# Delta-rule attention and two MLPs on one core: K and q of the first chunks loaded in natural layout and transposed by quadrants, norms in fewer instructions, a new order

## The chip, the cores and the metric

The kernel runs on one core of a Trainium2 chip. The time is that of one execution in device microseconds, from launch to end; the median of several runs is given. Lower is better.

## The reference

Three parts follow each other. The first is an attention with a state that a delta rule updates, for 4 batches of 8 heads, 768 tokens, head dimension 48:

```python
k_n = k / (np.linalg.norm(k, axis=-1, keepdims=True) + 1e-06)
for t in range(S):
    kt, vt, bt = (k_n[:, :, t], v[:, :, t], beta[:, :, t, None])
    y[:, :, t] = np.einsum('bhd,bhde->bhe', q[:, :, t], state)
    v_old = np.einsum('bhde,bhd->bhe', state, kt)
    state = state + bt[:, :, :, None] * np.einsum('bhd,bhe->bhde', kt, vt - v_old)
```

Its output, 3072 tokens of 384 values, goes through two MLPs (384 to 2048 to 384): the first with a quadratic bend between -1 and 1 in place of a ReLU, the second with h * clip(h + 3, 0, 6) / 6. All is float32.

## The kernel before

The 768 tokens are cut into 12 chunks of 64. For a chunk, all 32 (batch, head) pairs are worked on at once; they lie on two halves of the partitions, 16 units u in each half. `front(c)` (L1465) does what does not need the state: it loads K in natural layout into KN[c % 2] (`load_kv`, L847), computes the norms (`norms`, L872), brings K and q into the transposed layout (KTT, QQ), multiplies K by K and by q (`products`, L942), inverts the triangular matrix of the chunk (`inverse`, L1003) and scales V. `chain(c)` (L1133) then takes the state: it subtracts what the state holds already (K times state), applies the inverse (E, G), adds to the state (E, KN: the last reader of KN[c % 2]) and makes y, whose two halves, high and low part, go to XB for the MLP. A float32 product on TensorE is done as two matrix instructions; the MLPs split each operand into a high and a low part and do three products.

For chunks 0 to 3 (c < ct = 4) the transposed layout of K and q is made by TensorE. `load_tok` (L800) loads K a second time and q into padded buffers ST (for chunks 0 and 1 also into four buffers that lie in G, cleared by `zero`), two transfers of 96 KB for each half hb. `transposes` (L914) then turns 128 tokens and pairs at once: four instructions of `nc.tensor.transpose` against the identity IDN, for each of K and q and of two hb; ScalarE or VectorE copies the bank to KTT or QQ. From chunk 4 on, `block_transposes` (L827) does it on VectorE from STB, which lies in the same memory as ST.

The inverse ends in a forward substitution: `steps` (L1018) issues two small instructions for each of 15 rows (31 from chunk 4 on), `TMP = TL * DL` (L1029) and `TL = TL - TMP` (L1034), one after another. Whether VectorE or GpSimd takes them is set by `tpool`, which lists chunks 2 to 11.

`wload` (L1276) converts the weights of an MLP block f from HBM words into a high and a low part (L1313 to L1325), some on ScalarE, some on VectorE, a few on GpSimd. MLP block 0 works on chunk 0 alone, block 1 on chunk 1, each later block on two chunks. `mg` says how many weight blocks block 0 is ahead before block 1 is interleaved.

Nothing runs in the order of the text. `Plan.op` records every operation with an assumed duration and a priority, `Plan.emit` (L341) simulates the engines and picks an order from the priorities, and `rearrange` (L590) then moves single operations to other places (`MOVES`) and other engines (`TAKEN`). The priority of a stage of a chunk is

```python
def pri(c, name):
    return c + PR[name] - (PR["first"] if c == 0 else 0) + (PR["off"][c] if c < len(PR["off"]) else 0) + PR["pg"].get((c, name), 0)
```

and the lower one goes first. `hyst` is the time in nanoseconds for which the simulation holds quadrant work (products of 64 x 64 or 32 x 32 tiles) back so that two such groups can stand together; groups named in `urg` (inverse, state update, u, y) are not held. Where TensorE waits in the opening, the plan fills it with products that nobody reads (`fill`, on GH).

Of the kernel before, what the change touches and what calls it, by code (L numbers as in the profile page):

```python
# [19 lines left out]
RATIO = 0.0672  # L20
# [3 lines left out]
PR = dict(tl=53.380307, tp=0.183739, pk=1,  # L24
          pg={(0, 'chain'): 15.406015, (0, 'inv'): -0.97796, (0, 'kv'): -3.174274, (0, 'lv'): 1.308145, (0, 'norm'): 1.19811, (0, 'pm'): -0.151105,
              (0, 'prod'): 0.777632, (0, 'tok'): -0.552347, (0, 'tr'): 1.012284, (0, 'y'): -0.443861, (1, 'chain'): 0.042635, (1, 'inv'): -1.23228,
# [17 lines left out]
          dx=0.998118, sx=65.747392, dl=753.315017, ms=('act', 'dve'), wd=4, fm=-64.663392, aw=('act', 'dve', 'pool'), mg=10, fl=4553.24511,  # L44
          off=(-9.521246, 4.24236, 3.60679, -11.476239), mb=(29.802453, -3.591307), slots=2, fast=(0,), slate=0, mk=0, hm=303.25043, kv=-20.5097,
          tok=-4.956834, norm=-3.403349, tr=-1.523895, prod=7.676092, pm=9.657382, inv=-7.144682, sv=17.887724, w=-1.449, chain=2.315386, y=0.495043,
          wl=6.676133, wls=0.156421, mp=-1.413011, lv=-24.378343, first=-2.104309, bias=-134.594302, fill=3000,
# [4 lines left out]
MOVES = ((19, 0), (18, 19), (11, 18), (78, 11), (20, 78), (12, 20), (21, 12), (58, 82), (38, 5), (83, 38), (39, 83), (6, 17), (56, 6), (22, 56),
# [1662 lines left out]
```

## Time and profile before

| | us |
|---|---|
| median of 3 runs | 1007.03 |
| lowest and highest run | 1006.11, 1007.99 |
| profiled execution | 1007.33 |
| its span, first to last instruction | 1005.50 |
| TensorE busy in the span | 968.4 |
| VectorE, ScalarE, GpSimd busy | 613.6, 483.5, 299.8 |

The profiled execution is the one that the rows below come from; 1.83 us of its time lie outside the span. The busy time of TensorE covers its matrix instructions with modelled ends, and an engine's share over the whole span mixes an opening, in which weights are converted and the first chunks prepared, with a long stretch of MLP work. [...]

### The profile page before, as it was taken

How to read it: one execution, taken by the hardware profiler on the slowest of the kernel's cores; microseconds unless marked ns; L12 is line 12 of the kernel's file. 1: busy time of each engine (PE TensorE's matmuls, PEld its weight loads, DVE VectorE, ACT ScalarE, POOL GpSimd, SP SyncE). 2: the span in 40 equal slices, each digit the busy share in tenths (PEclk: the TensorE clock that was granted, in tenths of full speed). 3: DMA queues.
4: the chain of work that ended last, by engine and by line, in shares of the span. 5: the costliest groups of instructions: out<-in, count | busy, mean ns of one | idle time of the engine just before them, and what ended most of it. 6: DMA issues, size and time to landing. Idle time of an engine off the chain costs nothing.

```text
span 1005.5 us, 27383 instructions
## 1 busy us (share of the span) xinstructions
PE 968.4 (96%) x11540; PEld 834.8 (83%) x11540; DVE 613.6 (61%) x1161; ACT 483.5 (48%) x934; POOL 299.8 (30%) x663
## 2 busy tenths in 40 slices
PE   5788899999999999999999999999999999999998
PEld 4667889978777887887887888998989898989998
DVE  4999788887778687778555886434242324242422
ACT  5769666556455465544436774323232323232422
POOL 2112443758557685685811110210000000000000
PEclk9768999999999999999999999999999999999999
DMA  7774433433333233222023665003200200200000
GB/s 152 190 189 115 105 80 64 79 54 57 52 86 58 43 51 93 39 45 70 20 97 102 214 194 157 1 1 95 63 32 1 63 32 14 66 16 1 33 1 32
DMA packets 208460, 71.78 MB, mean 71 GB/s; under 512 B 154960, under 2 KB 204240, under 8 KB 208336
## 3 DMA queue, kind: packets, MB, share of 16 engines
q1 hardware_dynamic: 205376, 69.44, 28.8%
q8 instruction: 90, 1.47, 0.6%
q10 hardware_dynamic: 2960, 0.59, 0.3%
q14 instruction: 34, 0.28, 0.1%
HBM read 53.68 MB, written 14.16 MB: 67 GB/s over the span
## 4 chain that ended last, share of the span: by engine, by line
PE 84%; DVE 7%; ACT 4%; DMA 2%; issue 1%; SPq 1%; POOL 0%; ACTq 0%; DVEq 0%; POOLq 0%
PE bank L759 84%; DVE TBS L1313 1%; DMA RAWL<-in_moe_w_out_dram 1%; DVE WLA L717 1%; ACT TBS L1316 1%; ACT GF L1377 0%; DVE GF L1379 0%; ACT GF L1378 0%; DVE RAWL L1319 0%; DMA KN<-in_k_dram 0%; DVE KQ L1319 0%; ACT WLA L728 0%; DVE TL L1034 0%; DVE SM L884 0%; DMA RAWR<-in_moe_w_out_dram 0%
## 5 line engine op out<-in xcount | busy, mean ns | idle before, releaser
L759 PE MATMUL bank<-XB,WLA 128*128 128x512 f32 (+1 forms) x1404 | 327.7, 380 | 4.8 <-ACT GF L1377 2.7
L759 PEld LDWEIGHTS bank<-XB,WLA 128*128 128x128 f32 x1404 | 250.1, 190 | 55.0 <-DVE GF L1379 6.1
L1383 DVE SCALAR_TENSOR_TENSOR GF<-GF,bank 128x512 f32<-128x512 f32 x96 | 66.0, 688 | 159.6 <-ACT GF L1382 159.6
L1382 ACT ACTIVATE GF<-bank 128x512 f32<-128x512 f32 x96 | 57.4, 599 | 171.2 <-PE bank L759 161.7
L1029 POOL TENSOR_TENSOR TMP<-TL,DL 128x126 f32<-128x126 f32 (+25 forms) x278 | 111.4, 401 | 60.6 <-DVE DL L1087 34.1
L1034 POOL TENSOR_TENSOR TL<-TL,TMP 128x126 f32<-128x126 f32 (+25 forms) x278 | 118.0, 425 | 21.7
L759 PE MATMUL bank<-GH,WLA 128*128 128x512 f32 (+1 forms) x504 | 120.0, 366 | 1.4 <-ACT RAWR L728 1.4
L759 PE MATMUL bank<-XB,WLB 128*128 128x512 f32 (+1 forms) x468 | 109.3, 377 | 0.5 <-DVE GF L1379 0.3
L728 ACT ACTIVATE GH<-GF 128x512 fp32r<-128x512 f32 (+1 forms) x120 | 69.0, 578 | 74.5 <-DVE GF L1379 38.2
L759 PEld LDWEIGHTS bank<-GH,WLA 128*128 128x128 f32 x504 | 87.0, 191 | 16.3 <-ACT RAWR L728 1.6
L759 PEld LDWEIGHTS bank<-XB,WLB 128*128 128x128 f32 x468 | 83.2, 188 | 16.3 <-DVE GF L1379 0.7
L1377 ACT ACTIVATE GF<-bank 128x512 f32<-128x512 f32 (+1 forms) x112 | 59.5, 532 | 74.8 <-PE bank L759 61.6
L717 DVE TENSOR_TENSOR GL<-GF,GH 128x512 fp32r<-128x512 f32 (+1 forms) x109 | 72.3, 664 | 34.5 <-ACT GH L728 26.9
L1379 DVE SCALAR_TENSOR_TENSOR GF<-bank,GF 128x512 f32<-128x512 f32 (+1 forms) x112 | 67.8, 609 | 38.3 <-ACT GF L1378 34.5
L1378 ACT ACTIVATE GF<-GF 128x512 f32<-128x512 f32 (+1 forms) x112 | 63.4, 568 | 2.6
L759 PE MATMUL bank<-GL,WLA 128*128 128x512 f32 (+1 forms) x252 | 64.6, 366 | 0.0
L717 POOL TENSOR_TENSOR GL<-GF,GH 128x512 fp32r<-128x512 f32 (+1 forms) x27 | 30.6, 1132 | 103.5 <-ACT GH L728 83.5
L759 PEld LDWEIGHTS bank<-GL,WLA 128*128 128x128 f32 x252 | 43.8, 190 | 7.2
L759 PE MATMUL bank<-WLA,GH 128*128 128x384 f32 x220 | 46.6, 349 | 3.1 <-ACT WLA L728 3.1
L759 PEld LDWEIGHTS bank<-WLA,GH 128*128 128x128 f32 x220 | 39.9, 193 | 5.3 <-ACT WLA L728 3.9
L759 PE MATMUL bank<-GH,WLB 128*128 128x512 f32 (+1 forms) x168 | 39.0, 363 | 0.0
L759 PEld LDWEIGHTS bank<-KQ 48*64 48x64 f32 x1152 | 28.5, 152 | 9.5 <-ACT KQ L728 3.9
(196 smaller groups left out, 1431.0 us busy)
## 6 DMA issues: line engine op xcount, KB each, us to landing
XB<-X SPq DMA_DIRECT2D x36, 256.0 KB, 4.4
X<-XB SPq DMA_DIRECT2D x30, 256.0 KB, 2.5
KQ<-in_moe_w_out_dram SPq DMA_DIRECT2D x16, 384.0 KB, 4.1
KQ<-in_moe_w_in_dram SPq DMA_DIRECT2D x16, 384.0 KB, 4.7
KN<-in_k_dram SPq DMA_DIRECT2D x24, 192.0 KB, 3.6
RAWL<-in_moe_w_out_dram SPq DMA_DIRECT2D x12, 384.0 KB, 5.4
out_dram<-E SPq DMA_DIRECT2D x24, 192.0 KB, 1.9
RAWL<-in_moe_w_in_dram SPq DMA_DIRECT2D x24, 144.0 KB, 3.9
```

The costliest lines, as they stand in the source:

```text
L717: alts[e] = (d, lambda e=e: ENG[e].tensor_tensor(out=val(out), in0=val(in0), in1=val(in1), op=op))
L728: lambda: nc.scalar.activation(out=val(out), in_=val(in_), func=AF.Copy, scale=scale))
L759: nc.tensor.matmul(o, l, r, start=start, stop=stop, skip_group_check=skip)
L1029: P.op(te, d, lambda t=t, s=s, r0=r0, a0=a0, a1=a1, m=m: ve.tensor_tensor(out=t[:, a0:a1], in0=TL[:, r0 + a0:r0 + a1, s:s + 1].to_broadcas ...
L1034: P.op(te, d, lambda t=t, s=s, r0=r0, a0=a0, a1=a1: ve.tensor_tensor(out=TL[:, r0 + a0:r0 + a1, 0:s], in0=TL[:, r0 + a0:r0 + a1, 0:s], in1 ...
L1313: P.op("dve", 67 + 0.53 * n, lambda s_=s_, hw=hw: W.tensor_scalar(out=s_, in0=hw, scalar1=-2147483648, scalar2=None, op0=ALU.bitwise_and), ...
L1316: P.op("act", 166 + n, lambda s_=s_, lw=lw: nc.scalar.activation(out=s_.bitcast(I16).rearrange("p (n t) -> p t n", t=2)[:, 0], in_=lw.bitc ...
L1377: P.op("act", da, lambda: nc.scalar.activation(out=gf, in_=ps, func=AF.Relu, scale=0.5, bias=0.5), r=hkeys(hb, hv), w=gk, prio=mp)
L1378: P.op("act", da + 48, lambda: nc.scalar.activation(out=gf, in_=gf, func=AF.Square), w=gk, r=gk, prio=mp)
L1379: P.op("dve", 1.06 * n + 60, lambda: nc.vector.scalar_tensor_tensor(out=gf, in0=ps, scalar=1.0, in1=gf, op0=ALU.max, op1=ALU.min), r=hkeys ...
L1382: P.op("act", da, lambda: nc.scalar.activation(out=gf, in_=ps, func=AF.Relu, scale=1.0 / 6.0, bias=0.5), r=hkeys(hb, hv), w=gk, prio=mp)
L1383: P.op("dve", 1.06 * n + 60, lambda: nc.vector.scalar_tensor_tensor(out=gf, in0=gf, scalar=1.0, in1=ps, op0=ALU.min, op1=ALU.mult), r=hkey ...
```

## The change

The second load of K is gone. K is read out of KN, which the norms and the state update use too, and q is loaded in the same natural layout into QN: for chunks 0 and 1 into the memory of G, for chunks 2 and 3 into that of ST. `transposes` multiplies quadrants of 64 x 64 by a quadrant of the identity, 16 products for a call and two more where the last unit has no 64 columns. The condition `c < PR["ct"]` is as before, so this holds for chunks 0 to 3. The norms take the root with a bias in place of a maximum, and a Relu on ScalarE stands for two steps on VectorE. The clearing of the four buffers is gone. All settings, MOVES and TAKEN are from a new search; among them tpool now lists chunks 0 and 1 too, and hyst, mg and the priorities differ.

```diff
-RATIO = 0.0672
+RATIO = 0.08603
...
-          tok=-4.956834, norm=-3.403349, tr=-1.523895, prod=7.676092, pm=9.657382, inv=-7.144682, sv=17.887724, w=-1.449, chain=2.315386, y=0.495043,
-          wl=6.676133, wls=0.156421, mp=-1.413011, lv=-24.378343, first=-2.104309, bias=-134.594302, fill=3000,
-          tpool=(2, 3, 4, 5, 6, 7, 8, 9, 10, 11), hc=1, halves=1, biasa=873.603855, b16=(0, 1, 2, 3), hyst=1599.18963, fgap=589.297285, me=300,
...
+          aw=('act', 'dve', 'pool'), mg=12, fl=5004.56908, off=(0.407006, 1.099343, -4.45226, -17.582803), mb=(30.430605, -8.43156), slots=2,
+          fast=(0,), slate=0, mk=0, hm=3.441689, kv=-22.656238, tok=-1.658581, norm=-5.921339, tr=-7.667599, prod=-5.210624, pm=1.784778,
+          inv=-4.833225, sv=23.14785, w=-1.449, chain=14.336995, y=7.703994, wl=4.177815, wls=0.059205, mp=-7.898513, lv=-19.500437, first=14.033467,
+          bias=-130.893752, fill=3000, tpool=(0, 1, 2, 3, 4, 5, 6, 7, 8, 9, 10, 11), hc=1, halves=1, biasa=873.608597, b16=(0, 1, 2, 3),
+          hyst=9693.5056, fgap=513.276091, me=10, c3=('act', 'pool'), back=19928.2499, dh=100, margin=0.001, umargin=244.041264,
...
-    extra = [gw[:, 512 * i:512 * i + 512] for i in range(4)]
-    ST += [x.rearrange("p (a x) -> p a x", a=NP) for x in extra]
+    QN = [x.rearrange("p (u d) -> p u d", d=D) for x in (gw[:, 0:U * D], gw[:, 1024:1024 + U * D], ST2.rearrange("p n a x -> p (n a x)")[:, 0:U * D])]
...
-    def load_tok(c, hb, src):
...
+    def load_q(c):
+        P.tag = f"tok c{c} q"
+        for dl in range(2):
+            act = c == 0
+            P.dma(lambda dl=dl, act=act: (nc.scalar if act else nc.sync).dma_start(out=QN[min(c, 2)][SH[dl]], in_=nat(q, c, dl)), CH * U, CH * U * D * 4, eng="act" if act else "sp",
...
-        P.op("dve", 82, lambda: W.tensor_scalar_max(s(1), s(0), 1e-30), r=["sm0"], w=["sm1"], prio=pr, port=("dve",))
-        P.op("act", 200, lambda: nc.scalar.activation(out=s(2), in_=s(1), func=AF.Sqrt), r=["sm1"], w=["sm2"], prio=pr)
+        P.op("act", 200, lambda: nc.scalar.activation(out=s(2), in_=s(0), func=AF.Sqrt, scale=1.0, bias=1e-30), r=["sm0"], w=["sm2"], prio=pr)
         P.op("dve", 170, lambda: W.reciprocal(out=s(3), in_=s(2)), r=["sm2"], w=["sm3"], prio=pr)
-        P.op("dve", 82, lambda: W.tensor_tensor(out=s(4), in0=s(1), in1=s(3), op=ALU.mult), r=["sm1", "sm3"], w=["sm4"], prio=pr, port=("dve",))
-        P.op("dve", 82, lambda: W.tensor_tensor(out=s(5), in0=s(2), in1=s(4), op=ALU.add), r=["sm2", "sm4"], w=["sm5"], prio=pr, port=("dve",))
-        P.op("dve", 82, lambda: W.tensor_scalar(out=NRM[st], in0=s(5), scalar1=0.5, scalar2=1e-6, op0=ALU.mult, op1=ALU.add),
-             r=["sm5"], w=[("nrm", st)], prio=pr, port=("dve",))
+        P.op("act", 130, lambda: nc.scalar.activation(out=s(5), in_=s(2), func=AF.Relu, scale=0.5, bias=1e-6), r=["sm2"], w=["sm5"], prio=pr)
+        P.op("dve", 82, lambda: W.scalar_tensor_tensor(out=s(4), in0=s(0), scalar=0.5, in1=s(3), op0=ALU.mult, op1=ALU.mult), r=["sm0", "sm3"], w=["sm4"], prio=pr, port=("dve",))
+        P.op("dve", 82, lambda: W.tensor_tensor(out=NRM[st], in0=s(5), in1=s(4), op=ALU.add), r=["sm5", "sm4"], w=[("nrm", st)], prio=pr, port=("dve",))
...
-    def transposes(c, hb, i, is_k):
+    def transposes(c, hb, is_k):
...
+        src, nm, x = (KN[st], "kn", st) if is_k else (QN[min(c, 2)], "qn", min(c, 2))
+        flat = src.rearrange("p u d -> p (u d)")
         def pe():
-            for p in range(NP):
-                nc.tensor.transpose(bk.tile[0:112, p * 128:(p + 1) * 128], ST[i][:, p, 0:112], IDN)
+            for a in range(NP):
+                for g in range(2):
+                    for dl in range(2):
+                        o = a * 128 + g * CH
+                        x0 = D * (g * NK + hb * NP + a)
+                        x1 = min(x0, U * D - 64)
+                        mm(bk.tile[SH[dl], o:o + CH], flat[SH[dl], x1:x1 + 64], IDN[SH[dl], SH[dl]])
+                        if x1 < x0:
+                            mm(bk.tile[HD[dl], o:o + CH], flat[SH[dl], x0:x0 + D], IDN[SH[dl], SH[dl]])
...
+        if c < PR["ct"]:
+            load_q(c)
         for hb in range(2):
             if c < PR["ct"]:
-                ik = load_tok(c, hb, k)
-                iq = load_tok(c, hb, q)
-                transposes(c, hb, ik, True)
-                transposes(c, hb, iq, False)
+                transposes(c, hb, True)
+                transposes(c, hb, False)
             products(c, hb)
...
-    for i in range(4):
-        zero(ST[2 + i], [("st", 2 + i)], 470)
```

## Rows read from the trace of the kernel before

**Rows 1.** Windows of the whole core; after the stretch, its length, each engine busy (instructions)

```profile
0.00:67.05 67.05, 45.87 (x969) 36.93 (x969) 52.19 (x155) 41.45 (x84) 10.82 (x30) 0.78 0.74 170
67.05:128.00 60.95, 51.29 (x1291) 47.28 (x1290) 53.69 (x116) 47.04 (x99) 21.10 (x44) 0.88 0.54 124
128.00:600.00 472.00, 469.20 (x7248) 384.77 (x7248) 360.62 (x670) 265.43 (x539) 258.08 (x582) 1.00 0.35 80
600.00:1005.50 405.50, 402.01 (x2034) 365.87 (x2034) 147.09 (x222) 129.56 (x215) 9.78 (x7) 1.00 0.12 38
```

**Rows 2.** The chain of waits, first 30 us: start, length, what

```profile
4.46 4.41 DMA KN<-in_k_dram
```

**Rows 3.** Timeline of all engines, first 20 us: start, length, engine, line, operation, count

```profile
11.18 0.83 ACT L878 ACTIVATE X<-KN 128x768 f32<-128x768 f32 x1
...
14.24 0.17 DVE L889 TENSOR_TENSOR SM<-SM 128x16 f32<-128x16 f32 x1
...
14.45 0.18 DVE L890 TENSOR_TENSOR SM<-SM 128x16 f32<-128x16 f32 x1
...
14.46 3.72 PE L759 MATMUL bank<-KQ 48*64 48x128 f32 x96 [2.52 <-DVE SM L889]
...
16.90 0.42 DVE L966 TENSOR_TENSOR X<-bank,ND 128x256 f32<-128x256 f32 x1 [0.29 <-ACT KQ L974]
```

**Rows 4.** Timeline of TensorE, first 200 us

```profile
8.90 2.19 PE L921 MATMUL bank<-IDN,G 128*112 128x128 f32 x8 [0.92 <-DMA G<-in_k_dram]
...
20.74 0.62 PE L921 MATMUL bank<-IDN,G 128*112 128x128 f32 x4
...
40.62 1.10 PE L921 MATMUL bank<-IDN,ST 128*112 128x128 f32 x4
...
54.67 2.03 PE L759 MATMUL bank<-E,KN 64*48 64x48 f32 x64
...
67.05 4.48 PE L759 MATMUL bank<-XB,WLA 128*128 128x256 f32 x18
...
100.19 2.90 PE L759 MATMUL bank<-KQ,E 48*48 48x64 f32 x128
...
106.18 0.94 PE L759 MATMUL bank<-E,KN 64*48 64x48 f32 x64 [1.08 <-DVE YS L1248]
...
147.97 2.03 PE L759 MATMUL bank<-KQ,E 48*48 48x64 f32 x128
```

**Rows 5.** Timeline of TensorE, 300 to 390 us

```profile
303.24 0.97 PE L759 MATMUL bank<-GL,WLA 128*128 128x512 f32 x3
...
329.70 0.84 PE L759 MATMUL bank<-GL,WLA 128*128 128x512 f32 x3
```

**Rows 6.** Windows of VectorE, instructions on TMP alone

```profile
0.00:67.05 67.05, 11.67 (x53) 0.78 0.74 170
...
sum 1005.50, DVE 12.98; mean DVE 3.25
```

**Rows 7.** Timelines of VectorE and GpSimd, first and last substitution steps

```profile
23.23 0.17 DVE L1029 TENSOR_TENSOR TMP<-TL,DL 128x15 f32<-128x15 f32 x1
...
34.61 1.03 DVE L1034 TENSOR_TENSOR TL<-TL,TMP 128x15 f32<-128x15 f32 x1
...
53.49 0.18 DVE L1029 TENSOR_TENSOR TMP<-TL,DL 128x15 f32<-128x15 f32 x1
...
71.24 0.18 DVE L1034 TENSOR_TENSOR TL<-TL,TMP 128x15 f32<-128x15 f32 x1
...
34.52 1.07 POOL L717 TENSOR_TENSOR WLA<-RAWL,WLA 128x384 fp32r<-128x384 f32 x1 [5.12 <-ACT WLA L728]
...
103.48 0.33 POOL L1029 TENSOR_TENSOR TMP<-TL,DL 128x15 f32<-128x15 f32 x1 [4.27 <-DVE DL L1058]
...
115.55 0.23 POOL L1034 TENSOR_TENSOR TL<-TL,TMP 128x15 f32<-128x15 f32 x1
```

More of the change, by code (lines that the diff above doesn't have):

```diff
@@ L52 @@
[L52 removed]
[226 rows of a table removed]
[L279 to L283 removed]
+PR = dict(tl=293.787129, tp=4.414826, pk=1,
+          pg={(0, 'inv'): 1.288053, (0, 'kv'): 0.012598, (0, 'lv'): 0.099566, (0, 'norm'): 0.108177, (0, 'pm'): 0.514614, (0, 'prod'): -0.32987,
+              (0, 'sv'): 1.411888, (0, 'tok'): -0.072668, (0, 'tr'): -1.082274, (0, 'y'): -0.781211, (1, 'kv'): 1.47192, (1, 'lv'): -0.339201,
+              (1, 'norm'): -0.136947, (1, 'prod'): 0.637285, (1, 'tok'): 0.268505, (1, 'tr'): 0.19817, (10, 'chain'): -0.961739,
[5 rows of a table added]
+              (2, 'prod'): -0.173157, (2, 'tok'): 0.350917, (2, 'tr'): -0.823694, (2, 'y'): -1.283838, (3, 'chain'): 0.413498, (3, 'inv'): -2.52562,
+              (3, 'norm'): 0.386412, (3, 'pm'): -1.27796, (3, 'prod'): 1.357839, (3, 'sv'): 1.063503, (3, 'tok'): 0.428693, (4, 'chain'): -1.120612,
[9 rows of a table added]
+              (9, 'tr'): 2.980542, (9, 'y'): 0.26363}, dx=1.022497, sx=41.802129, dl=318.887832, ms=('act', 'dve'), wd=4, fm=9941.86254,
+          aw=('act', 'dve', 'pool'), mg=12, fl=5004.56908, off=(0.407006, 1.099343, -4.45226, -17.582803), mb=(30.430605, -8.43156), slots=2,
[3 more added lines that the diff above has]
+          hyst=9693.5056, fgap=513.276091, me=10, c3=('act', 'pool'), back=19928.2499, dh=100, margin=0.001, umargin=244.041264,
+          urg=('inv', 's', 'u', 'y'), sw=(217, 95), ad=('act', 'dve'), dp=('dve',), ct=4, dg=('dve', 'pool'), dw=('dve', 'pool'), pq=190)
@@ new lines @@
+MOVES = ((4, 0), (6, 4), (12, 6), (5, 12), (18, 5), (7, 18), (66, 3), (14, 66), (131, 14), (34, 131), (187, 11), (13, 187), (525, 13), (383, 33),
[227 rows of a table added]
+TAKEN = dict(dve=(36, 49, 52, 157, 176, 352, 359, 492, 500, 605, 611, 616, 757, 779, 979, 1131, 1156, 1158, 1302, 1305, 1307, 1437, 1501, 1649, 1650,
+             1679, 1822, 1958, 2184, 2207, 2377, 2490, 2643, 2711, 2815, 2885, 2886, 2888, 3022, 3033, 3055, 3066, 3093, 3097, 3101, 3246, 3248,
+             3263, 3269, 3286, 3295, 3320, 3331, 3342, 3353, 3386, 3397, 3452, 3497, 3542, 3554, 3560, 3578, 3616, 3723,), pool=(32, 37, 50, 181,
+             194, 379, 747, 780, 902, 1041, 1043, 1048, 1185, 1339, 1700, 1713, 2232, 2234, 2480, 2593, 2765, 2924, 3012, 3034, 3056, 3287, 3310,
+             3398, 3420, 3453, 3510, 3564, 3600, 3608, 3609, 3639, 3674, 3684, 3694, 3724, 3754, 3764,))
@@ L795, in zero @@
         P.op("pool", dur, lambda: nc.gpsimd.memset(ap, 0.0), w=keys)
-    stage = [0]
-    def load_tok(c, hb, src):
-        P.tag = f"tok c{c} h{hb}"
-        if c < 2:
-            i = (0 if hb == 0 else 2 + 2 * c) + stage[0] % 2
-        else:
-            i = stage[0] % NST
-        stage[0] += 1
-        for b in range(2):
-            ap = src[2 * b + hb, :, c * CH:(c + 1) * CH, :].rearrange("h s d -> s h d")
-            dst = ST[i][64 * b:64 * b + 64].rearrange("p a (e x) -> p (a e) x", e=2)[:, :, 0:D]
-            act = c == 0 and hb == 1
-            P.dma(lambda ap=ap, dst=dst, act=act: (nc.scalar if act else nc.sync).dma_start(out=dst, in_=ap), CH * H, CH * DM * 4, eng="act" if act else "sp",
-                  w=[("st", i, b)], r=[("st", i)], prio=pri(c, "tok") - (0.01 if c == 0 and hb == 0 else 0.0), bulk=c > 0)
-        return i
+    def load_q(c):
[3 more added lines that the diff above has]
+            P.dma(lambda dl=dl, act=act: (nc.scalar if act else nc.sync).dma_start(out=QN[min(c, 2)][SH[dl]], in_=nat(q, c, dl)), CH * U, CH * U * D * 4, eng="act" if act else "sp",
+                  w=[("qn", min(c, 2), dl)], pre=[("st", 0), ("st", 1)] + [("stb", d, f, t) for d in range(2) for f in range(2) for t in range(2)] if c >= 2 else [], prio=pri(c, "tok"), bulk=c > 0)
     def load_blocks(c, src, nm):
@@ L824, in load_blocks @@
                     P.dma(lambda ap=ap, dst=dst: nc.sync.dma_start(out=dst, in_=ap), 32 * U, 32 * U * 4 * n,
-                          si=490, w=[("stb", dl, f, th)], pre=[("st", i, b) for i in range(2) for b in range(2)], prio=pri(c, "tok"), bulk=True)
+                          si=490, w=[("stb", dl, f, th)], pre=[("qn", 2, dl) for dl in range(2)] + [("st", 0), ("st", 1)], prio=pri(c, "tok"), bulk=True)
     def block_transposes(c):
@@ L918, in transposes @@
         pr = pri(c, "tr")
+        src, nm, x = (KN[st], "kn", st) if is_k else (QN[min(c, 2)], "qn", min(c, 2))
+        flat = src.rearrange("p u d -> p (u d)")
         def pe():
-            for p in range(NP):
-                nc.tensor.transpose(bk.tile[0:112, p * 128:(p + 1) * 128], ST[i][:, p, 0:112], IDN)
+            for a in range(NP):
[7 more added lines that the diff above has]
+                            mm(bk.tile[HD[dl], o:o + CH], flat[SH[dl], x0:x0 + D], IDN[SH[dl], SH[dl]])
         if is_k:
-            P.op("pe", 400, pe, load=0.85, ni=8, r=[("st", i, 0), ("st", i, 1), "idn"], w=[bk], pre=[("kt", st, hb)], alloc=bk, prio=pr)
+            P.op("pe", 880, pe, load=0.6, ni=64, tiled=True, r=[(nm, x, 0), (nm, x, 1), "idn"], w=[bk], pre=[("kt", st, hb)], alloc=bk, prio=pr)
             ks = slice(hb * NP, (hb + 1) * NP)
@@ L929, in transposes @@
         else:
-            P.op("pe", 400, pe, load=0.85, ni=8, r=[("st", i, 0), ("st", i, 1), "idn"], w=[bk], pre=[("qt", st, hb)], alloc=bk, prio=pr)
+            P.op("pe", 880, pe, load=0.6, ni=64, tiled=True, r=[(nm, x, 0), (nm, x, 1), "idn"], w=[bk], pre=[("qt", st, hb)], alloc=bk, prio=pr)
             o = QQ[st][0:112].rearrange("p (b h a) s -> p h a b s", b=2, h=2)[:, hb]
@@ L1096, in inverse @@
         P.op("dve", 620, lambda: nc.vector.transpose(out=NH, in_=TT), r=["dl"], w=["nh"], prio=pr)
-        early_st = [("st", 2 + 2 * st + i, b) for i in range(2) for b in range(2)] if c < 2 else []
+        early_st = [("qn", c, dl) for dl in range(2)] if c < 2 else []
         for g in range(2):
```

13 lines of the change are left out of this document (removed), and 483 rows, old and new, of tables (MOVES, pg).

## The prediction

> **What bounds it now.** I read the windows first, cut at the first MLP product and at the point from which TensorE stays full [rows 1]. From 128 us to the end TensorE is busy 871.21 of 877.5 us at full granted clock, so there the time is its work and nothing else: only fewer or shorter TensorE instructions help. Ahead of 128 us it sits idle 21.18 + 9.66 = 30.8 us, and the mean clock is 0.78 and 0.88 of full. In that opening VectorE is the fullest engine, 105.88 of 128 us, with ScalarE at 88.49. The reader is to see two regimes. In the opening, the chain of chunk 0 and the conversion of the weights share VectorE and ScalarE, and what comes sooner there shifts the full stretch forward. Behind it, every TensorE instruction added costs its length.
>
> The chain of waits and the timeline then show the first microseconds. The second half of K for the norms is on that chain until 8.87 us [rows 2]. The square starts at 11.18, the products at 14.46 and the scaling of X at 16.90 [rows 3]. On TensorE the first MLP product is at 67.05 us, so chunk 0 needs 50 us from X to there [rows 4].
>
> **What the change does to this, step by step.** The sum is made against the profiled execution: span 1005.50 us, 1007.33 with what lies around it, 0.30 over the median of 1007.03.
>
> *Loads.* The second reading of K goes, 16 transfers of 96 KB (64 x 8 rows of 192 B, four a chunk); q comes in half as many, twice as large. For chunk 0, that leaves four transfers in place of ten ahead of the products. K could land some 2 to 2.4 us sooner if its second half is issued at about 2 us and takes the 4.41 us it took [rows 2]; SP then no longer holds the V and RAWL loads behind K and q. The four removed clears on GpSimd have no reader in the new form and hide behind the loads. I take -2 us, between -4.7 (square straight after K, at 6.5 in place of 11.18) and 0.
>
> *Transposition.* A call was four transposing instructions; eight took 2.19 us at the start, a later four 0.62 [rows 4], ends included. A call is now 16 or 18 quadrant products, 32 or 36 matrix instructions, since each fp32 product is two here (the 48 products from 14.46 us on are 96 instructions [rows 3]). The nearest row is y, whose 128 instructions of 64 columns take 2.03 us at full clock and 2.90 at a lower one [rows 4], 16 and 23 ns each: 0.54 and 0.77 us for the mean call of 34. But y takes the four quadrants in turn and the new calls only the two on the diagonal, so up to twice that is possible, 1.08 and 1.54. Against 0.62 and 1.1 that is -0.3 to +0.5 us a call. I take +0.4, near the upper end, because only two quadrants work. Chunk 0 has four calls ahead of its products: +1 us, since two of them hide behind loads. Chunk 1's four fall into idle TensorE time. Those of chunks 2 and 3 move to where TensorE is nearly full: eight times 0.4, +3 us, bounds -2.4 and +4.
>
> [...] The rows agree that leaving quadrants costs: three products right behind a quadrant group take 0.97 us, three others 0.84 [rows 5]. That is 0.13 us; with as much on entering, an estimate, 0.26 a group. If all 16 calls stood alone this would be +4.2 us; next to the products, which are quadrant work too, nothing. I take +0.5.
>
> *Norms.* Of the small VectorE steps behind the first reciprocal three become two, and the maximum ahead of the root goes. A step costs 0.21 us from start to start (14.24 to 14.45 [rows 3]), the maximum with its wait about as much; -0.4 us for chunk 0, inside the -2, and two steps of 0.17 us of VectorE's time for each chunk. The added Relu on ScalarE runs beside the reciprocal and costs nothing unless ScalarE is busy then; its price would be 0.2 us.
>
> *The new wait.* K for chunk 2 is now transposed out of KN[0], which chunk 0's state products (E, KN) read at 54.67 us; before, the last transposition of chunk 2 was at 40.62 [rows 4]. Chunk 3 likewise waits for chunk 1, 106.18 us. Behind the waiting load on SP are weight loads; behind the waiting transposition on TensorE is whatever the order put there. Chunk 2's norms needed the same KN[0] before, so its products gain no new predecessor but about 4 us of transposition and copying. I take 0: idle TensorE time covers it. Without that cover it is the second rival.
>
> *Substitution of chunks 0 and 1.* tpool now holds 0 and 1, so their 60 instructions, 12.98 us of VectorE, go to GpSimd [rows 6]. On VectorE chunk 0 took from 23.23 to 35.64, 12.4 us, and chunk 1 from 53.49 to 71.42, 17.9 us. Chunk 2 on GpSimd took from 103.48 to 115.78, 12.3 us [rows 7]. Chunk 0's chain gains nothing by itself (bounds -2.5, 30 steps of the 0.33 us of the first row, an estimate, and +5.5, the 17.9 us of chunk 1); chunk 1's gains about 5.6 us.
>
> *What VectorE does with the room.* 11.67 of those 12.98 us lie ahead of 67.05 us [rows 6], where VectorE was busy 52.19 us [rows 1]. The new priorities also put chunk 0's chain (14.337 - 14.033 + 0.407 = 0.71) ahead of the weights (4.18); before, it was 10.30 against 6.68. Chunk 0's waits behind conversions shrink and the conversions still find time. Of the 11.67 us I give half, less what the longer GpSimd path loses: -5 us for the first MLP product (bounds -11.7 and 0). Behind it, chunk 1 comes sooner by its 5.6 us, but ScalarE, 47.04 of 60.95 us, keeps most of that: -2 us (bounds -6 and 0). The idle 9.66 us there is the room.
>
> *Order.* The planner's hold for quadrant work rises from 1.6 to 9.7 us, so that groups may be joined. It concerns three groups a chunk (two products, one K-state product); over chunks 4 to 11 that is 24 x 0.26 = 6.2 us at most, 0 at least. I take -1.5.
>
> Sum: -2 + 1 + 3 + 0.5 + 0 - 5 - 2 - 1.5 = -6.0, with chunk 0's extra transposition counted in the +1. That gives 1001.3 by the profiled execution and 1001 us by the median, 0.6% less. With every term at its bound it would reach from -4.7 - 1.2 - 2.4 - 2.5 - 11.7 - 6 - 6.2 = -34.7 to 2 + 4 + 4.2 + 5.5 = +15.7, 972 to 1023; they won't all fall on one side.
>
> **Rivals.** *GpSimd held up.* Mechanism: the moved substitution and VectorE's two-operand work block each other. The row for it: a step of 15 columns on VectorE took 1.03 us at 34.61, when GpSimd had begun a tensor product of 1.07 us at 34.52, and 0.17 at 23.23 [rows 7]. Against it: chunk 2's 30 steps took 12.3 us in all. In chunk 0's stretch VectorE is fuller. Its mean instruction in the opening is 52.19 / 155 = 0.34 us; if each of the 30 steps waited for one, chunk 0 would lose 10 us, and VectorE would lose what it gained. Then -2 + 1 + 3 + 0.5 + 10 - 2.5 - 1.5 = +8.5: 1015.5 us. It decides from 0.2 us a step on, where the 6 us are gone. [...] Chance 0.16.
>
> *The gain stops on the way.* The opening is shorter, but chunks 2 and 3 come no sooner because their K waits for KN, and TensorE runs out of the small blocks' MLP work ahead of block 2. Priced: the 7 us of the opening are given back, +3.5 of transposition and -1.5 of order remain: 1009. For it speaks 106.18 us, where chunk 1 frees KN[1]; 4.4 us of landing and four calls with copies, some 6 us, put the K of chunk 3 at about 117. Against it: the norms of chunk 3 needed the same rows. With part of it given back, no change. Chance 0.17.
>
> *All of VectorE's room reaches the chain.* -11.7 in place of -5 and -6 in place of -2: 990 us. For it: chunk 0's path from X to the MLP was 50 us, of which its 12.4 us of substitution and TensorE's few products are the smaller part. Against it: ScalarE stays as full. Chance 0.17.
>
> **How the numbers follow.** The forecast holds 0.50 with 995 to 1005 around 1001. Measured against 1007.03, a difference of 0.2%, 2 us, is about what can be told from no change. Faster: 0.17 + 0.48 from the forecast + 0.03 from the second rival = 0.68. Within 0.2%: 0.02 + 0.08 = 0.10. Slower: 0.16 + 0.06 = 0.22. The range from 989 to 1012 takes in the larger gain and the second rival, and leaves out the first one's 1015.5 and the tails.
>
> **What would show it.** The first MLP product on XB at 58 to 62 us; TMP and TL on GpSimd for chunks 0 and 1 in 11 to 14 us each; VectorE's busy time down by some 13 + 12 x 0.34 = 17 us; transposition calls of 0.5 to 1.1 us at full clock; the last stretch unchanged in length. It is wrong if chunk 0's 30 steps on GpSimd take over 18 us, if TensorE idles ahead of block 2, or if the full stretch behind 128 us grows by more than the 4 us of transposition.

## The result, and the profile after

The changed kernel takes 1017.71 us (median of 4 runs, 1014.0 to 1019.88) against 1007.39 for the one before on the same chip: a ratio of 1.010, interval 1.0076 to 1.0124. On another chip it took 1015.48 against 1007.08, 1.0082 (1.0068 to 1.0096). It is 8 to 10 us slower, where 1001 was forecast and 1012 was the upper end of the range.

The profiled execution is the fastest one, 1014.0 us with a span of 1012.2; it is compared with the span of 1005.5. The windows with the cuts of [rows 1]; behind the engines stand the granted clock as a share of full speed, the DMA share and GB/s:

```profile
0.00:67.05 67.05, 49.01 (x1334) 42.08 (x1334) 45.20 (x100) 43.86 (x88) 30.52 (x84) 0.85 0.77 177
67.05:128.00 60.95, 51.78 (x1381) 47.65 (x1385) 51.95 (x106) 45.94 (x99) 19.05 (x46) 0.92 0.37 90
128.00:600.00 472.00, 464.12 (x7253) 378.55 (x7244) 356.21 (x654) 259.90 (x531) 255.56 (x582) 1.00 0.35 76
600.00:1012.20 412.20, 408.79 (x2064) 371.10 (x2062) 148.64 (x225) 136.10 (x224) 15.03 (x11) 1.00 0.13 41
```

Ahead of 128 us TensorE idles 27.2 us in place of 30.8. Between 128 and 600 us it idles 7.9 in place of 2.8, and the last stretch is 6.7 us longer because that much work is still to do at 600 us. Behind 128 us TensorE has 872.9 us of work in place of 871.2, and 11.3 us of idle time in place of 6.3. So of the 6.7 us, 1.7 are work that the opening leaves over and 5.0 are idle time where the granted clock is 1.00 and TensorE was full. The opening, which was to gain 6 us, gains nothing.

TensorE's groups by line, the calls of the transposition alone (instructions, busy us, mean ns, idle time before them); before, the sixteen calls took 10.2 + 3.7 = 13.9 us in 64 instructions:

```profile
L760 PE MATMUL bank<-IDN,KN 64*64 64x64 f32 (+1 forms) x272 | 12.2, 263 | 8.7 <-DMA KN<-in_k_dram 7.0 <-DVE XB L1252 1.3 <-issue 0.4
L760 PE MATMUL bank<-IDN,ST 64*64 64x64 f32 (+1 forms) x136 | 5.8, 244 | 0.0
L760 PE MATMUL bank<-IDN,G 64*64 64x64 f32 (+1 forms) x136 | 4.7, 219 | 0.3 <-DMA G<-in_q_dram 0.3
```

Together 22.7 us, 8.8 more. With TensorE's busy time of 973.7 against 968.4, all its other work became 3.5 us shorter; 2.9 of that are the filling products that nobody reads (40 in 14.6 us before, 38 in 11.7 after). So the account of the 6.7 us of span is: calls +8.8, other work -3.5, idle time ahead of 130 us 30.9 to 27.6 (-3.3), from 130 to 600 us 2.8 to 7.5 (+4.7).

TensorE's timeline, the rows that answer to [rows 3] and [rows 4]:

```profile
6.22 3.88 PE L760 MATMUL bank<-IDN,KN 64*64 64x64 f32 x68 [6.22 <-DMA KN<-in_k_dram]
...
11.28 2.24 PE L760 MATMUL bank<-IDN,G 64*64 64x64 f32 x68 [0.34 <-DMA G<-in_q_dram]
...
15.14 3.09 PE L760 MATMUL bank<-KQ 48*64 48x128 f32 x94 [1.62 <-ACT KQ L729]
...
61.23 3.71 PE L760 MATMUL bank<-IDN,KN 64*64 64x64 f32 x68 [1.32 <-DVE XB L1252]
...
64.87 1.69 PE L760 MATMUL bank<-XB,WLA 128*128 128x256 f32 x12
...
111.80 0.94 PE L760 MATMUL bank<-E,KN 64*48 64x48 f32 x64
...
131.00 0.98 PE L760 MATMUL bank<-XB,WLA 128*128 128x256 f32 x6 [0.59 <-DVE GF L1376]
...
141.90 1.69 PE L760 MATMUL bank<-XB,WLA 128*128 128x256 f32 x12 [0.59 <-DVE GF L1376]
...
144.06 0.62 PE L760 MATMUL bank<-XB,WLA 128*128 128x256 f32 x3 [0.47 <-ACT GF L1374]
...
156.99 0.32 PE L760 MATMUL bank<-KQ,E 64*48 64x64 f32 x6 [0.57 <-issue]
...
191.63 0.62 PE L760 MATMUL bank<-XB,WLB 128*128 128x256 f32 x3 [0.53 <-ACT GF L1374]
```

The reader is to see five things. Two calls take 2.24 us at full clock (from 11.28 us, granted clock 1.00) and 3.71 at a lower one (from 61.23 us, granted clock 0.50 up to 64.0 us, 0.55 over the two calls): 1.1 and 1.9 us each, the doubled bounds of the prediction and more. The first two, at 6.22 us, took 3.88 with no lower clock on record there (1.00). The products start at 15.14, later than 14.46 before (14.52 in the profile of the second chip), and wait for a copy of transposed q. The first MLP product is at 64.87, 2.2 us sooner, with two calls for K of chunk 2 directly ahead of it. Chunk 1's state products are at 111.80, where they were at 106.18: chunk 1 comes later, not sooner. And from 130 us on the MLP products wait half a microsecond at a time for the eviction that makes GF, five times and 2.7 us up to 200 us (before, 0.26 and 0.47 us, twice).

### The profile page after: what moved, and what is told of

The parts are those of the page before. It is cut to its first block, busy times and chain, and to the rows that moved or that the text cites. A ratio compares the mean times of both kernels' runs of the same rounds, so it can differ in the third digit from the quotient of the medians.

```text
span 1012.2 us, 28323 instructions
## 1 busy us (share of the span) xinstructions
PE 973.7 (96%) x12018; PEld 839.4 (83%) x12018; DVE 602.0 (59%) x1083; ACT 485.8 (48%) x941; POOL 320.2 (32%) x722
## 4 chain that ended last, share of the span: by engine, by line
PE 86%; DVE 5%; DMA 3%; ACT 2%; POOL 2%; issue 2%; SPq 1%; DVEq 0%; ACTq 0%; POOLq 0%
PE bank L760 86%; DMA RAWL<-in_moe_w_in_dram 1%; DMA KN<-in_k_dram 1%; POOL TMP L1026 1%; POOL TL L1031 1%; DVE GF L1376 1%; ACT GF L1374 1%; DVE WLA L718 1%; SPq L1293 0%; DMA RAWL<-in_moe_w_out_dram 0%; DVE RAWL L1316 0%; DVE TBS L1310 0%; DMA E<-in_beta_dram 0%; DVE X L963 0%; ACT GF L1375 0%
## 5 line engine op out<-in xcount | busy, mean ns | idle before, releaser
L1026 POOL TENSOR_TENSOR TMP<-TL,DL 128x126 f32<-128x126 f32 (+25 forms) x308 | 124.8, 405 | 68.5 <-DVE DL L1084 27.2
L1031 POOL TENSOR_TENSOR TL<-TL,TMP 128x126 f32<-128x126 f32 (+25 forms) x308 | 123.7, 402 | 24.0
L729 ACT ACTIVATE GH<-GF 128x512 fp32r<-128x512 f32 (+1 forms) x116 | 66.4, 576 | 72.4 <-PE bank L760 30.6
L760 PE MATMUL bank<-WLA,GH 128*128 128x384 f32 x195 | 38.8, 340 | 0.0
L760 PE MATMUL bank<-KQ 48*64 48x64 f32 (+1 forms) x1152 | 31.3, 248 | 6.0 <-ACT KQ L729 2.9
```

Source lines behind the costliest of these rows:

```text
L729: lambda: nc.scalar.activation(out=val(out), in_=val(in_), func=AF.Copy, scale=scale))
L760: nc.tensor.matmul(o, l, r, start=start, stop=stop, skip_group_check=skip)
L1026: P.op(te, d, lambda t=t, s=s, r0=r0, a0=a0, a1=a1, m=m: ve.tensor_tensor(out=t[:, a0:a1], in0=TL[:, r0 + a0:r0 + a1, s:s + 1].to_broadcas ...
L1031: P.op(te, d, lambda t=t, s=s, r0=r0, a0=a0, a1=a1: ve.tensor_tensor(out=TL[:, r0 + a0:r0 + a1, 0:s], in0=TL[:, r0 + a0:r0 + a1, 0:s], in1 ...
```

## The experiments

All times are medians; each is held against the kernel before on its own chip (1006.7 to 1007.4). "Idle" is TensorE's idle time between 130 and 600 us in the profile, 2.8 before and 7.5 after; "issue" is the time in which TensorE waits for nothing that the profile shows, 2.2 us in 4 places before, 8.6 in 12 after.

**The calls, in either kernel.** The same sixteen calls, of the other kind of instruction on the same tiles; what they leave in the bank isn't laid out as the products want it, the work is the same.

```diff
 # e1: the changed kernel
-            for a in range(NP): ... mm(bk.tile[SH[dl], o:o + CH], flat[SH[dl], x1:x1 + 64], IDN[SH[dl], SH[dl]])
+            for p in range(NP):
+                x0 = D * (hb * NP + p)
+                nc.tensor.transpose(bk.tile[0:112, p * 128:(p + 1) * 128], flat[:, x0:x0 + 112], IDN)
 # e2: the kernel before
-                nc.tensor.transpose(bk.tile[0:112, p * 128:(p + 1) * 128], ST[i][:, p, 0:112], IDN)
+                for e in range(2):
+                    for b in range(2):
+                        o = p * 128 + e * CH
+                        mm(bk.tile[SH[b], o:o + CH], ST[i][SH[b], p, CH * e:CH * e + 64], IDN[SH[b], SH[b]])
```

> The changed kernel in its own order; only the 16 transposition calls of chunks 0 to 3 are four transposing instructions again in place of 32 or 36 quadrant instructions (they read the same tiles; K and q in the transposed layout are other values). Theory 1, the quadrant calls cost the time by their own length (six calls in the full stretch at about 0.6 us more, two slow ones in front of the first MLP product) and by the instruction supply of TensorE: 1008 to 1011 us, and TensorE's idle time put down to issue falls from 8.6 us to about 3. Theory 2, the new order and settings are the slower part: 1015 to 1019. Theory 3, the substitution on GpSimd is: 1015 to 1019.

> The kernel before in its own order; only the 16 transposition calls are 32 quadrant instructions each, on the diagonal quadrants as in the changed kernel (their values land in other places). Theory 1: slower, but less than the 10 us, since twelve of the sixteen calls stand where TensorE idles: 1009 to 1013. Theory 2: 1007 to 1008.5. Theory 3: 1007 to 1008.5.

e1: 1012.74 us, ratio 1.005 (1.0035 to 1.0065), idle 7.0, issue 7.3. e2: 1011.59, 1.0044 (1.0029 to 1.0058), idle 5.1, issue 6.8. The calls cost 3 to 5 us in the new order and 4.4 in the old one. In e2 they are busy for as long as in the changed kernel:

```profile
L759 PE MATMUL bank<-IDN,ST 64*64 64x64 f32 x384 | 17.3, 244 | 8.2 <-issue 3.2 <-DMA ST<-in_q_dram 2.8 <-DVE XB L1258 1.5
L759 PE MATMUL bank<-IDN,G 64*64 64x64 f32 x128 | 5.3, 240 | 1.1 <-DMA G<-in_k_dram 1.1
```

That is 22.6 us, 8.7 more than before. The last of them ends at 111.7 us (122.5 in the changed kernel), so none lies in the full stretch, and the first MLP product comes at 71.09 us, 4.0 later than before. TensorE from 128 us to the end, in e1 and in e2 (window, length, busy time, instructions; clock and DMA behind them):

```profile
128.00:1009.70 881.70, 871.21 (x9212) 1.00 0.25 60
128.00:1009.20 881.20, 872.50 (x9291) 1.00 0.25 60
```

In e2's profile, 3.6 us of span longer than before, the opening leaves 1.3 us more work behind it, and idle time behind 128 us is 8.6 in place of 6.3. e1's 5.6 us over the kernel before are not the calls: in its profile, 4.1 us longer, TensorE has the same 871.2 us of work behind 128 us, and the idle time there is 10.4 us. So all of e1's longer span is idle time behind the opening.

**The search.** Both kernels without MOVES and TAKEN, as the planner alone orders them.

```diff
-        self.rearrange()
```

> The kernel before without its hand-written moves and engine choices: the order is the planner's. It is the base for the next run; theory 1 and 2 say nothing of its own time, I expect 1010 to 1025.

> The changed kernel without its moves and engine choices. Theory 1, the structure is slower: by 5 to 12 us over the kernel before without its moves. Theory 2, the slower part is what the search added: as fast as or faster than the kernel before without its moves.

e3: 1008.6, 1.001 (0.9997 to 1.0023), idle 2.1. e4: 1016.02, 1.009 (1.007 to 1.011), idle 7.3. The moved operations do little in either; the distance is there without them.

**The substitution.** In e5 the changed kernel's steps run on VectorE for chunks 0 and 1, in e6 those of the kernel before on GpSimd. Every place in the order stays.

```diff
 # e5
-        ve = ENG[te]
+        ve = nc.vector if c < 2 else nc.gpsimd
 # e6
-        ve = ENG[te]
+        ve = nc.gpsimd
```

> The changed kernel with the substitution of chunks 0 and 1 on VectorE, as before, each step in the place of TensorE's order that it has now; all else as changed. Theory S (GpSimd's substitution costs the part that the calls leave open, some 5.5 us: 1017.7 less 1012.7 was the calls): about 1012 us, and the idle time of TensorE in 130 to 200 us falls from 4.5 to about 1 us. Rival O (the order and its settings cost it, the substitution on GpSimd is hidden or gains): within 2 us of the changed kernel, 1015 to 1019. Rival V (VectorE is the engine the opening runs short of, so the move gains): 1020 or more.

> The kernel before with the substitution of chunks 0 and 1 on GpSimd and nothing else; TensorE's order is that of before. Theory S: 1010 to 1013 us. Rival O: within 2 us of before, 1005.5 to 1009. Rival V: 1002 to 1005, since VectorE gives up about 23 us of work in the first 115 us.

e5: 1014.08, 1.0062 (1.0041 to 1.0084), idle 7.6: 1.4 us below the changed kernel's 1015.48, 3.6 below its 1017.71; the intervals overlap. e6: 1007.38, 1.0002 (0.9987 to 1.0016), idle 2.5. Theory S falls, and so does V: 11.7 us of room on VectorE were worth nothing in the old order.

**The settings.** Each structure ordered by the planner alone with the other's PR and RATIO.

> The changed kernel's loads, quadrant calls and norms, but ordered by the planner alone with the settings of before (priorities, costs, hold times, and the substitution of chunks 0 and 1 on VectorE). Theory S and rival O both want about 1012 us, only the calls being left of what costs (1008.6 of the old structure by its planner alone, with some 4 us for the calls); O wants it also where the substitution alone moved nothing. If the K loads tied to KN, the calls' places or the changed loads cost the open part (theory K): 1016 to 1018, as the changed code by its planner alone with its own settings (1016.0).

> The kernel before, its loads, calls and norms, ordered by the planner alone with the settings of the changed kernel (the substitution of chunks 0 and 1 on GpSimd among them). Rival O: 1013 to 1016 us, the loss of the settings without the calls. Theory S: the same 1012 to 1016 where the single move above also lost. Theory K: within 2 us of the old structure by its planner alone, 1006 to 1010.

e7: 1019.52, 1.0112 (1.0089 to 1.0135), idle 7.0. e8: 1044.74, 1.0362, idle 25. Settings fit one structure and are no part that can be moved alone. e8 can't be read as a loss of these settings where they belong. e7 speaks against the settings as the cause, but only weakly, since old settings are as foreign to the new structure.

**Both moves back, a shifted stream, the norms.** e9 is the changed kernel again (1015.48). e10 is e1 and e5 together. In e11 sixteen idle quadrant products stand ahead of the call for the first half of chunk 0's K; e12 is the kernel before with the new norms.

```diff
 # e11
+            if c == 0 and hb == 0 and is_k:
+                for _ in range(16):
+                    mm(bk.tile[SH[0], 0:CH], IDN[SH[0], SH[0]], IDN[SH[0], SH[0]])
 # e12: two steps fewer on VectorE, as in the change (not shown)
+        def roots():
+            nc.scalar.activation(out=s(2), in_=s(0), func=AF.Sqrt, scale=1.0, bias=1e-30)
+            nc.scalar.activation(out=s(5), in_=s(2), func=AF.Relu, scale=0.5, bias=1e-6)
...
```

> The changed kernel itself, on the chip of the next three kernels, so that they can be held against it without another chip between. 1015 to 1019 us by the earlier runs (1014.0 to 1019.9).

> The changed kernel with both moves taken back that lost time alone: the calls again of four transposing instructions, and the substitution of chunks 0 and 1 again on VectorE. If the two losses add (calls some 5 us, substitution some 3.5 us): 1008 to 1010 us, and nearly all of the changed kernel's loss is told by these two. If the substitution's loss is only the run-to-run place of the instruction stalls (the single move left the profiled span at 1012): as the old calls alone, 1012 to 1014, and 4 to 6 us stay with the loads, the norms and the order.

> The changed kernel with 16 more quadrant products of the identity ahead of its first call (64 more TensorE instructions with their weight loads and register moves, about 0.3 to 0.6 us; their result is overwritten), so that every later instruction stands elsewhere in TensorE's instruction stream. Theory I (the stalls in which TensorE waits for nothing the profile shows, 8.6 us in 12 places, are the supply of instructions, set by where the dense calls stand in that stream): the stalls move to other places and their sum changes by 1 us or more, and the time by as much. Rival P (they belong to the places in the program: the first instruction behind a certain wait): the same places, 8 to 9 us, and the time 0.3 to 0.6 us longer than the changed kernel.

> The kernel before with the norms of the change alone (two VectorE steps fewer in each chain of steps, a ScalarE step more). The prediction's price is 0.4 us of the first chain, which stands ahead of TensorE's wait of 2.5 us for SM: 1006 to 1007 us. If the chain behind takes it back as it took back the GpSimd substitution's room: 1007 to 1008. Above 1008.5 the ScalarE steps are in the way of an eviction.

e10: 1013.82, 1.0066 (1.0053 to 1.0079), idle 6.8. The two don't add: with the calls and the substitution undone, 6.7 us are left. e12: 1007.71, 1.0007 (0.9998 to 1.0015): the norms gain nothing. e11: 1018.42, 1.0113 (1.0098 to 1.0127), 2.9 us above e9 where 0.3 to 0.6 were expected for the products. The waits of TensorE, the row of e9 (us in total, places, longest):

```profile
PE bank L760 <- issue: 10.0, 12, 2.3
```

and that of e11:

```profile
PE bank L760 <- issue: 6.3, 7, 1.9
```

The stalls moved, as theory I had it: of the one at 50.94 us and the two at 41.97 and 45.97 in e9, e11 shows one at 46.22. But the run did not hold the rest still. TensorE's timeline has the sixteen products, 32 matrix instructions, as one row:

```profile
7.99 3.51 PE L760 MATMUL bank<-IDN 64*64 64x64 f32 x31
```

They took 3.5 us in place of the 0.3 to 0.6, at a point on which chunk 0 waits: its products start at 18.2 us in place of 14.5, and the first MLP product comes at 68.90 in place of 64.55. The 2.9 us at the end are less than the delay put in, so they say nothing of the place in the stream, and what the stalls cost stays open. The changed kernel itself came out at 1017.71 us on one chip and 1015.48 on another; differences of 1 to 2 us between kernels of the new structure (e5, e10, e14) don't tell causes.

**K tied to KN.** In the order before, the calls for K of chunk 2 ran at 29.46 and 36.75 us and those of chunk 3 at 66.10 and 74.73; out of KN they must follow the state products of chunk 0 and chunk 1. In e13 and e14 the two calls for K of chunk 2 go behind chunk 1's products; in e15, e16 and e18 the calls go in the kernel before to where the tie puts them, as list operations on the finished order:

```diff
+        for tags, anchor, before in [(("tr c2 h0 kTrue", "tr c2 h1 kTrue"), "prod c1 h1", False)]:   # e13, e14
+            ...   # e15, e16: ahead of "H1 b0 f0"; e18: and chunk 3's behind the first "inv c2"
+            self.order = rest[:n] + mv + rest[n:]
```

> The changed kernel with the two calls for K of chunk 2 moved from the place directly ahead of the first MLP product (3.71 us at the low clock, from 61.23 us) to the place behind the products of chunk 1, where TensorE runs 28 filling products that serve nothing (6.64 us from 30.23 us). There KN still holds K of chunk 0, so chunk 2 is computed with chunk 0's K: the same work on other data. Theory P (K tied to KN took these calls out of TensorE's waiting time and put them on the path): the first MLP product at 61 to 62 us, and 1011.5 to 1013 us against 1015.5 to 1017.7, 3 to 4 us less. Rival Q (the opening isn't what sets the end; what is gained ahead of the MLP is lost in the waits for evictions behind 130 us): within 1 us of the changed kernel.

> The same move, and all sixteen calls made of four transposing instructions as before (the layout of their result differs, the work behind them is the same). Theory P: the old calls alone gave 1012.7, of which the two calls ahead of the MLP should still cost 1.7 us: 1010.5 to 1011.5. What is then left over 1007.2, some 4 us, is in the order behind 130 us (4.8 us of idle time there against 1.0). Rival Q: 1012 to 1013.5. Below 1009: the two moves together would tell the whole loss.

> The kernel before, with its calls of four transposing instructions, and only the two calls for K of chunk 2 (with their evictions) moved from 30 to 43 us, where TensorE waits and runs fillers, to the place directly ahead of the first MLP product (the staging buffer holds the second half of K by then, so the first call takes that). Theory P: two calls of 0.44 us from start to start at full clock, 0.85 to 1.1 us at the low one: 1008.5 to 1010. Rival Q: 1006 to 1008.

> The kernel before with the sixteen calls made of quadrant products and the two calls for K of chunk 2 moved ahead of the first MLP product, as in the changed kernel. Theory P: the quadrant calls at their old places gave 1011.6; with two of them now in TensorE's way for 3.7 us: 1014 to 1016, which is the changed kernel's time, by the calls and their places alone. Rival Q: 1011 to 1012.5.

> The kernel before with its old calls, and the calls for K of chunk 2 (ahead of the first MLP product) and of chunk 3 (behind the first products of chunk 2's inverse, some 45 us later than before) at the places that the tie to KN leaves them; the rest of the order stays, so the staging buffer holds other halves of K by then. Chunk 2's alone gave 1007.8 against 1006.7. Theory T: 1010 to 1012 us and the idle time behind 130 us up from 2.5 to 5 or more. Rival Q: 1007 to 1009, idle time there below 3.5 us.

e13: 1020.95, 1.014 (1.0119 to 1.0161), idle 9.7. e14: 1013.77, 1.0072, as e10. The 3.71 us ahead of the first MLP product were no price: with the calls gone, TensorE waits there for XB, so that the product comes at 64.99 in place of 64.87. In e13:

```profile
64.99 1.70 PE L769 MATMUL bank<-XB,WLA 128*128 128x256 f32 x12 [2.30 <-ACT XB L738]
```

Why e13 is 3 to 6 us slower than the changed kernel was not found; of the 2.2 us more that it idles between 130 and 600 us, 1.8 are waits put down to "issue" (4.1 us in place of 2.3). In the kernel before the late places cost about 1 us, which is hardly clear of noise. e15: 1007.83, 1.0009 (0.9997 to 1.0021), idle 2.5; its first MLP product, 67.05 before, moved by as much:

```profile
65.74 2.81 PE L930 MATMUL bank<-IDN,ST 128*112 128x128 f32 x12 [1.39 <-DVE XB L1264]
68.21 2.06 PE L768 MATMUL bank<-XB,WLA 128*128 128x256 f32 x8
```

e18: 1008.16, 1.0009 (1.0 to 1.0018), idle 2.7. e16: 1011.98, 1.0057 (1.0038 to 1.0077), idle 5.8, no more than e2. Theory P and, with e18, theory T fall: set by hand into the old order, the tie is worth 1 us (0 to 1.8), not 4.

> The changed kernel ordered by the planner alone with its own settings (that was 1016.0 us, with 7.3 us of TensorE's idle time between 130 and 600), with one line different: the planner does not count KN among what the calls for K of chunks 2 and 3 wait for, so they go to where the order of before had them (chunk 2's into the opening, chunk 3's ahead of the first MLP product) and read what KN holds then, K of the chunk two earlier. The quadrant calls stay. Theory T (K tied to KN costs the open 4 us, through the order behind the opening): 1010.5 to 1013 us, idle time behind 130 us at 3 to 5 us. Rival Q (the tie costs nothing, the searched order's waits have another cause): 1014.5 to 1017.5.

```diff
-            P.op("pe", 880, pe, ..., r=[(nm, x, 0), (nm, x, 1), "idn"], ...
+            P.op("pe", 880, pe, ..., r=[(nm, x, 0), (nm, x, 1), "idn"] if c < 2 else ["idn"], ...
```

e17: 1032.6, idle 20.6. The planner put the calls where the order of before has them, and the order as a whole became bad, as in e8. It tells nothing of the tie.

No version beat the kernel before; e3, e6, e12 and e15 equal it within their intervals.

## Why the prediction was wrong

The sums add up; set beside what each term measured:

| term | forecast | measured |
|---|---|---|
| loads, norms | -2 | 0: products 15.14 against 14.46 us; norms alone +0.6 (-0.2 to +1.5) |
| transposition, with entering and leaving quadrants | +4.5 | +4.4 in the old order (e2), +3 to +5 in the new (e1) |
| the new wait | 0 | +0.9 (0 to 1.8; e18, old order) |
| substitution, VectorE's room | -7 | 0 (e6), first MLP product only 2.2 us sooner |
| order | -1.5 | +4 to +6, what is left over |

*Loads* failed first in time. K did come sooner: its call starts at 6.22 us, the square at 8.03 in place of 11.18. But q now ends later, and chunk 0's products wait for the last copy of it:

```profile
14.49 0.60 ACT L729 ACTIVATE KQ<-bank 112x512 f32<-112x512 f32 x1
```

This copy ends at 15.09 us. The sum had followed K and the norms to the products and not the other operand.

*Transposition* held, in its sum more than in its working. A call took the doubled bound (1.1 us) at full clock and more than it (1.9) at the low one, so the sixteen calls took 8.8 us more, of which e2 shows 4.4 in the time. The prediction had put the calls of chunks 2 and 3 where TensorE is nearly full; they all end by 122.5 us, so their length is not what stands behind 128 us. The first bound named, 0.54 us, was not close: at granted clock 1.00 the calls from 11.28 us on, on two quadrants, took 2.24 us for 68 instructions, 33 ns each, and y, on four, 2.03 us for 128 [rows 4], 16 ns each. No run shows the +0.5 for entering and leaving quadrants by itself: [rows 5] have 0.13 us behind a quadrant group, the same on entering was an estimate, and e2 shows 4.4 us for the calls as a whole.

*VectorE's room* is the step that failed most. What was predicted of the engine came: chunk 0's steps ran from 23.42 us for 12.3 us on GpSimd, inside the 11 to 14 named. These are the first and last of them:

```profile
23.42 0.27 POOL L1026 TENSOR_TENSOR TMP<-TL,DL 128x15 f32<-128x15 f32 x1 [6.83 <-DVE DL L1055]
...
35.48 0.23 POOL L1031 TENSOR_TENSOR TL<-TL,TMP 128x15 f32<-128x15 f32 x1
```

Chunk 1's ran from 52.76 to 68.64, 15.9 us in place of 12.3. Here the first rival's mechanism shows, with VectorE busy for 83% of the stretch (52% in chunk 0's): seven of the 30 steps took 0.85 to 0.98 us, the others 0.21 to 0.53. Each of the seven began inside a VectorE instruction of two tiles that takes about 1 us, and ended 0.08 to 0.16 us after it. One of them, with the step behind it:

```profile
57.46 1.05 DVE L1316 SCALAR_TENSOR_TENSOR RAWL<-RAWL,TBS 128x768 int32<-128x768 int32 x1
57.76 0.90 POOL L1026 TENSOR_TENSOR TMP<-TL,DL 128x60 f32<-128x60 f32 x1
58.74 0.31 POOL L1031 TENSOR_TENSOR TL<-TL,TMP 128x60 f32<-128x60 f32 x1
```

That is some 4 us of one chunk, not the 10 us of that rival's price, and e6 shows that the whole move costs nothing. That the rival's 1015.5 us lies next to the measured time is luck.

VectorE's busy time fell by 11.6 us, less than the 17 named. The mistake was to turn an engine's busy time into time of the chain: the first MLP product came at 64.87, not at 58 to 62. e6 has the room without the rest and gains nothing at 1007.38. What the chain waits for besides VectorE is read from rows, and no run took any of it away alone: ScalarE's copy ahead of the products, 2.30 us for XB from ScalarE in e13, and loads of weights, which stand in the chain that ended last in the changed kernel:

```profile
46.72 4.42 DMA RAWL<-in_moe_w_in_dram
...
60.00 3.59 DMA RAWL<-in_moe_w_in_dram
```

*Order* had the wrong sign. Seven profiles of the changed structure by hand-moved order (changed, e1, e5, e9, e10, e11, e14) idle 6.8 to 7.6 us behind 130 us, with old and new calls, on either engine, and e13 9.7; the planner's own orders (e4, e7) 7.0 and 7.3. The old order idles 2.5 to 2.7 with old calls (e6, e12, e15, e18) and 5.1 to 5.8 with the new ones (e2, e16). By e1 and e10, with the tie taken off, some 4 to 6 us are left for the new order together with the natural loads; no run parts these two. TensorE's waits between 130 and 600 us (total, times, longest), first before, then after:

```profile
PE bank L759 <- DVE GF L1379: 1.4, 3, 1.0
PE bank L759 <- issue: 0.6, 2, 0.3
PE bank L759 <- ACT GF L1377: 0.5, 1, 0.5
...
PE bank L760 <- issue: 2.3, 3, 1.3
PE bank L760 <- ACT GF L1374: 1.5, 3, 0.5
PE bank L760 <- DVE GF L1376: 1.5, 4, 0.6
PE bank L760 <- DVE XB L1252: 1.0, 1, 1.0
```

Up to 200 us the waits for GF make most of it; over the whole stretch the waits put down to "issue" grow most. They rise by 1.7 us, those for GF by 1.1, those for XB from none to 1.5 (with two smaller rows, 0.3 and 0.2, not shown); in e1, with the old calls, issue is 2.9, GF 2.4, XB 1.1. The term had counted what joined groups of quadrant products save, 0.26 us each by that estimate, and no price for them. What the section on the hardware below shows of the supply of instructions is such a price; whether it comes from the longer hold was not tried. For GF, the timelines suggest that chunk 1's state products come 5.6 us later while the MLP of block 0 is taken early, so that later on there is less to put between two MLP products. This is argued; no run changed it alone.

The second rival was nearest, with its mechanism half right. The opening's gain is indeed given back and the calls cost what it said; the order's -1.5 that it kept should have been at least +4, which makes its 1009 into 1014.5. Its place, K waiting for KN, was wrong: that is 1 us. Of the signs named in advance, "the full stretch behind 128 us grows by more than the 4 us of transposition" is the one that showed.

Open stays why the planner, with either settings, can't fill the stretch behind 130 us in the new structure. The natural loads were never run alone in the old order. That order transposes chunk 2's K ahead of chunk 0's state products, so with K read out of KN it can't be kept as it is; with the places of e18 it could be, and this was not tried. So the loads stand beside the order as an untested cause.

## What to carry to other kernels

Room on the fullest engine need not be a gain: here 11.7 us of it on VectorE, given alone in e6, left 1007.38 us. Follow the chain to the next wait (here ScalarE's copies, XB and the loads of weights) and price the move by itself before it is counted. A change in the opening can cost in the full stretch: here 3.5 of the 4.7 us of new idle time lie between 130 and 200 us, behind the last of the new calls (122.5 us). An experiment that is to shift instructions and nothing else must not stand on the chain: e11's products put the first MLP product off by 4.4 us. Settings found for one structure can be far off under another (1044.7 us in e8, and 1032.6 with one dependency less), so a search's result can only be judged as a whole.

## What the runs showed of the hardware that was not expected

TensorE stalls without a releaser in runs of quadrant products: 8.6 us in 12 places in the changed kernel, 2.2 us in 4 before, 14 of these 16 inside a quadrant group. In the changed kernel stalls that follow each other closely stand 128 matrix instructions apart. TensorE's timeline, two places:

```profile
50.98 1.31 PE L760 MATMUL bank<-E,G 64*64 64x48 f32 x36 [0.51 <-issue]
...
55.54 0.27 PE L760 MATMUL bank<-KQ,E 64*48 64x64 f32 x4 [0.36 <-issue]
...
59.54 0.37 PE L760 MATMUL bank<-E,KQ 48*64 48x48 f32 x10 [0.21 <-issue]
...
121.73 0.73 PE L760 MATMUL bank<-IDN,KN 64*64 64x64 f32 x17 [0.37 <-issue]
...
125.45 0.43 PE L760 MATMUL bank<-DL,NH 32*32 32x32 f32 x26 [0.74 <-issue]
...
129.47 0.39 PE L760 MATMUL bank<-NH,LT 32*32 32x32 f32 x24 [0.39 <-issue]
```

Counted by the timeline, 988, 1116 and 1244 matrix instructions lie ahead of the first three and 2521, 2649 and 2775 ahead of the others: 128 (once 126) from one to the next, which with their weight loads is 256 instructions, and 3.7 to 4.6 us. The 128 instructions of y took 2.03 us at full clock [rows 4]. The trace also has a DMA queue q8 of the kind "instruction", in the changed kernel with 94 packets of 16384 bytes (packets, MB, share), where its 24036 matrix instructions and weight loads are 93.9 times 256:

```profile
q8 instruction: 94, 1.54, 0.6%
```

The closest two of them land 3.3 us apart. The 16 stalls of before and after, and all 132 in the twenty profiles, end 1.1 to 1.7 us after such a packet has landed; from this and the spacing I read that TensorE waits there for the supply of instructions. Such stalls take 2.2 us before, 6.8 with the quadrant calls alone (e2), 7.3 with the new order and the old calls (e1), 8.6 after. Since e2's calls all end by 111.7 us, none adds its length behind 130 us; of the 2.3 us more that it idles there, 1.7 are such stalls. How much of the changed kernel's 8 to 10 us they make is not shown: no run takes them away, and e11, which has fewer, delayed chunk 0 as well.
